# Block order of the first feed-forward layer: token tile 0 in three pieces, and one weight unit converted per block

## The chip, the cores and the metric

The kernel runs on one core of a Trainium2 chip. The metric is the device time of one execution in microseconds. The kernel before takes 804.77 us (median of three runs, 803.89 to 807.13).

## What is computed

Attention in which a query sees only the keys of its own hash bucket, then two feed-forward layers with different activations, on the 1536 tokens that attention puts out:

```python
q_bucket = np.sum((np.einsum('bhsd,dk->bhsk', q, proj) > 0) * 2 ** np.arange(6), axis=-1)   # k_bucket alike
scores = np.where(q_bucket[..., :, None] == k_bucket[..., None, :], scale * q @ k.T, -1e9)
attn_out = softmax(scores) @ v            # batch 2, 8 heads, 768 tokens, head_dim 64
x = attn_out.transpose(0, 2, 1, 3).reshape(1536, 512)
h = x @ w_in;  x = (h * np.cos(h)) @ w_out                 # layer 0: 512 -> 2048 -> 512
h = x @ w_in2; out = (h * np.tanh(log1p(exp(h)))) @ w_out2  # layer 1
```

The weights arrive as 64-bit floats.

## The kernel before, in words

`attention()` runs head by head. `moe()` then runs both layers, feature-major: the tokens are three tiles of 512 (t = 0, 1, 2), d_ff is 16 f-blocks of 128, and each pair of a tile and an f-block is one step of a long list, `uses` (lines 89 to 94), 48 steps for a layer. Tile 0 is finished in the middle of attention; the last pieces of x for tiles 1 and 2 (lines 394 and 397, on GpSimd) come with the last heads.

One pass of the loop at line 681 is called block n here. In it TensorE does h(n), twelve matmuls of w_in by x (line 171), and then o(n-4), twelve matmuls of w_out by the activation of block n-4 (line 667). Every operand is a sum of a high and a low part, so h takes high by high, high by low and low by high. h_mm takes the eight with w_in's high half first and the four with its low half last.

The activation of block n passes ScalarE and VectorE in turn: hs and a from the matmul's result (lines 181 and 183, block n), a on VectorE (193, block n), its absolute value and sine on ScalarE (189 and 190, block n+1), hs times cosine on VectorE (196, block n+1), and the split into gh on ScalarE (204) and gl on VectorE (206), block n+2. o(n) reads gh and gl two blocks later. The four h banks rotate; the four o banks have one buffer each.

A weight unit is w_in or w_out of one f-block: 512 KB of 64-bit floats, loaded by SP into one of five buffers (`load_w`), and converted in three blocks: cg on ScalarE (`conv1`, line 128), three integer operations on VectorE (`conv2`, lines 137, 139 and 142), the high half on ScalarE and the low half on GpSimd (`conv3`, lines 149 and 151). There are four cg buffers; the next unit's cg waits until GpSimd has released one. `due` hands out units in the order of their due times, two per block while n < 12 and one after that, once the slot is free (eight slots for w_in, eight for w_out). Four units, w_in 0 to 3, are converted during attention, and two more at its end. All engines run their queues in the order in which the code emits the instructions: stage_0, ophase, iter1 and split, finish, conv_mid, split_x, conv_next.

A run of steps of one tile adds up in the four o banks. When it ends, `finish` (line 610) empties them: by two copies on VectorE and two on ScalarE into a pa buffer in SBUF (lines 624 and 626), where more f-blocks of the tile are to follow, and by adds on VectorE (632, 641) where the tile is complete. In the kernel before, the runs of a layer are: tile 0, f 0 to 7; tile 1, f 0 to 7; tile 2, all 16; tile 1, f 8 to 15; tile 0, f 8 to 15.

Of the kernel before, what the change touches and what calls it, by code (L numbers as in the profile page):

```python
# [14 lines left out]
ALU = mybir.AluOpType  # L15
# [30 lines left out]
def lsh_moe_kernel(ctx: ExitStack, tc: tile.TileContext, q, k, v, proj, w_in1, w_out1, w_in2, w_out2, cst, out):  # L46
    nc = tc.nc
# [5 lines left out]
    NF = FF // 128  # L53
# [7 lines left out]
    NT3 = B * S // TT  # L61
    GRP = NF // 2

    def f32(ap):
        return ap.bitcast(F32)
# [18 lines left out]
    def slot(pool, part, i):  # L84
        return pool.tile([128, 2, 4, 128], F32R, name=f"w{part}_{i}")

    slots = [[slot(persist, 0, i) for i in range(NEARLY)], []]
    loads = [(wi, wo, f) for wi, wo in ((w_in1, w_out1), (w_in2, w_out2)) for f in range(NF)]
    uses = []
    for m in range(2):  # L90
        ts = list(range(NT3))[:: 1 if m == 0 else -1]
        for g, order in enumerate((ts, ts[::-1])):
            for t in order:
                uses += [(m, t, m * NF + g * GRP + f) for f in range(GRP)]
    NU = len(uses)
    LAG_O = 4
    last_use = {u[2]: n for n, u in enumerate(uses)}
# [26 lines left out]
    def conv1(u, step=None, g=None):  # L124
        if g is None:
            g = cv_p.tile([128, NCT, 128], F32, tag="g", name="cg", bufs=4)
        if step != 1:
            nc.scalar.activation(g, raw_t[u][:, :, :, 1].bitcast(F32), ACTF.Copy, scale=REBIAS)
        return u, g
# [15 lines left out]
    def conv3(st, step=None):  # L145
        (i, part), g = st
        w = slots[part][i % NW]
        if step != 1:
            nc.scalar.activation(w[:, 0], g, ACTF.Copy)  # L149
        if step != 0:  # L150
            nc.gpsimd.tensor_tensor(w[:, 1], g, f32(w[:, 0]), ALU.subtract)  # L151
# [59 lines left out]
    def conv_next(new):  # L211
        for st in pipe[1]:
            conv3(st)
        pipe[1] = pipe[0]
        pipe[0] = [conv1(u) for u in new]

    def conv_mid():
        return itertools.chain(*[conv2(st) for st in pipe[0]])
# [362 lines left out]
    def moe():  # L581
        mctx = ExitStack()
        with mctx:
            w_p = mctx.enter_context(tc.tile_pool(name="wslots", bufs=1))
            pools["g"] = mctx.enter_context(tc.tile_pool(name="g", bufs=4))
            pools["raw"] = mctx.enter_context(tc.tile_pool(name="raw2", bufs=RAWS2))
            ot_p = mctx.enter_context(tc.tile_pool(name="ot", bufs=3))
            pa_p = mctx.enter_context(tc.tile_pool(name="pa", bufs=1))
            ps_h = mctx.enter_context(tc.tile_pool(name="ps_h", bufs=4, space=PSUM))
            ps_o = mctx.enter_context(tc.tile_pool(name="ps_o", bufs=1, space=PSUM))  # L590
            part = [[pa_p.tile([128, TT], F32, name=f"pa{i}_{d}") for d in range(4)] for i in range(2)]
            O = []
            saved = {}
            for x in range(2):
                for i in range(len(slots[x]), NW):
                    slots[x].append(slot(w_p, x, i))
            LAG = LAG_O
            rest = []
            nxt["base"] = nxt["load"]
            for _ in range(RAWS2):  # L600
                load_w()

            def split_x(k):
                for _ in range(k):
                    if rest:
                        xh, xl, y = rest.pop(0)
                        nc.scalar.activation(xh, y, ACTF.Copy)
                        nc.vector.tensor_tensor(xl, y, f32(xh), ALU.subtract)

            def finish(n):  # L610
                m, t, li = uses[n]
                ps = n // GRP % (2 * NT3)
                opens = ps < NT3 - 1
                closes = ps >= NT3
                if not (opens or closes):
                    return
                for d in range(4):
                    s = O[d]
                    if opens:
                        if d == 0:  # L620
                            saved[t] = part[ps]
                        pp = saved[t][d]
                        if d % 2 == 0:
                            nc.vector.tensor_copy(pp, s)
                        else:
                            nc.scalar.activation(pp, s, ACTF.Copy)
                        continue
                    adds = t in saved
                    if m == 0:
                        if adds:  # L630
                            y = saved[t][d]
                            nc.vector.tensor_tensor(y, s, y, ALU.add)
                        else:
                            nc.scalar.activation(XH[t][d], s, ACTF.Copy)
                            nc.vector.tensor_tensor(XL[t][d], s, f32(XH[t][d]), ALU.subtract)
                            continue
                        rest.append((XH[t][d], XL[t][d], y))
                    else:
                        if adds:
                            y = saved[t][d]  # L640
                            nc.vector.tensor_tensor(y, s, y, ALU.add)  # L641
                        else:
                            y = ot_p.tile([128, TT], F32, tag="y", name="y")
                            if d % 2 == 0:
                                nc.vector.tensor_copy(y, s)
                            else:
                                nc.scalar.activation(y, s, ACTF.Copy)
                        b, j = divmod(t * 4 + d, J)
                        dst = out[b * S:b * S + S, :].rearrange("(p j) f -> p j f", j=J)
                        nc.sync.dma_start(out=dst[:, j, :], in_=y)  # L650
                if closes:
                    saved.pop(t, None)

            def ophase(n):
                m, t, li = uses[n]
                ps = n // GRP % (2 * NT3)
                first = n % GRP == 0 and ps != NT3
                last = n % GRP == GRP - 1 and ps != NT3 - 1
                if first:
                    O[:] = [ps_o.tile([128, 512], F32, tag=f"o{d}", name=f"o{d}") for d in range(4)]  # L660
                wo = slots[1][li % NW]
                gh, gl = G.pop(n)
                for d in range(4):
                    ds = slice(d * 128, d * 128 + 128)
                    for x, (wi, g) in enumerate(((0, gh), (1, gh), (0, gl))):
                        lhs, rhs = (wo[:, wi, d, :], g) if m == 0 else (g[:, ds], wo[:, wi].rearrange("p c f -> p (c f)"))
                        nc.tensor.matmul(O[d], lhs, rhs, start=(first and x == 0), stop=(last and x == 2))  # L667

            def due(n, most):
                new = []  # L670
                while nxt["unit"] < len(units):
                    i, part = u = units[nxt["unit"]]
                    ready = i < NW or last_use[i - NW] <= n - LAG * part + 1
                    must = n > 3 and due_at[u] <= n
                    if not ready or (len(new) >= most and not must):
                        break
                    new.append(u)
                    nxt["unit"] += 1
                return new

            for n in range(NU + LAG):
                if n == NU // 2:
                    iter1(n, last=True)
                    nc.scalar.preload_act_table_set("mish")
                if EARLY_H <= n < NU:
                    for _ in h_mm(n, ps_h.tile([128, TT], F32, tag="h", name="h")):
                        pass
                    stage_0(n)
                if n >= LAG:
                    ophase(n - LAG)  # L690
                if EARLY_H <= n < NU // 2:
                    iter1(n)
                elif n >= NU // 2:
                    split(n - 1)
                if n >= LAG and (n - LAG) % GRP == GRP - 1:
                    finish(n - LAG)
                for _ in conv_mid():
                    pass
                split_x(1)
                conv_next(due(n, 2 if n < 12 else 1))  # L700

    with tc.manual_schedule():
        attention()
        moe()
# [28 lines left out]
```

## Time and profile before

| | |
|---|---|
| median of three runs | 804.77 us |
| profiled execution | 804.95 us, of which 803.2 us from the first to the last instruction |
| TensorE busy | 780.2 us (97%) |
| VectorE, ScalarE, GpSimd busy | 538.2, 502.4, 304.3 us |
| attention | to about 262 us |
| the first layer's blocks | from 262.7 us; without a gap from 315 us |
| mean granted clock of TensorE | 0.989 |

A stretch's granted clock is the part of full speed that TensorE was given: 1.00 is 2.4 GHz, 0.50 is 1.2 GHz. Ends of matmuls are modelled, so distances between starts are read. DVE is VectorE, ACT is ScalarE, POOL is GpSimd, PE is TensorE.

### The profile page before, as it was taken

Reading aid. Unit: us, or ns where it says so; the run is one execution under the profiler, and the core shown is the slowest. Engines: PE = TensorE matmul, PEld = TensorE weight load, DVE = VectorE, ACT = ScalarE, POOL = GpSimd, SP = SyncE. Lnnn points to the kernel's source line nnn. Section 1 sums busy time; section 2 is a strip of 40 time slices with the busy share of each in tenths; the row PEclk is TensorE's granted clock in tenths of the full one; section 3 lists DMA queues with packets and bytes.
Section 4 is the critical chain, followed back from the end, with each engine's and each line's share of the span. In section 5 each row is a group of like instructions: output and inputs, shape, how many; then the busy total and the mean of one; then the engine's idle time right before and its main releaser. Section 6 shows DMA issues by size and latency. Waiting matters only on the chain.

```text
span 803.2 us, 11714 instructions
## 1 busy us (share of the span) xinstructions
PE 780.2 (97%) x4020; PEld 666.8 (83%) x4020; DVE 538.2 (67%) x940; ACT 502.4 (63%) x1002; POOL 304.3 (38%) x327
## 2 busy tenths in 40 slices
PE   8999999999999679999999999999999999999998
PEld 5889999999999467888888888888888888888886
DVE  5799899888897698448888546998412666611122
ACT  5899999998987576658777567774322443322120
POOL 4779999999875543002222101232200222200000
PEclk9999999999999889999999999999999999999999
DMA  7454354343320433003233001233200232001011
GB/s 226 102 152 114 104 155 111 104 128 86 84 56 16 162 106 104 1 0 100 84 106 103 29 1 53 79 105 108 76 1 12 94 105 79 0 1 53 0 53 52
DMA packets 38027, 62.36 MB, mean 78 GB/s; under 512 B 3664, under 2 KB 28368, under 8 KB 37968
## 3 DMA queue, kind: packets, MB, share of 16 engines
q1 hardware_dynamic: 37968, 61.63, 26.2%
q8 instruction: 31, 0.51, 0.3%
q14 instruction: 28, 0.23, 0.1%
HBM read 43.13 MB, written 3.15 MB: 58 GB/s over the span
## 4 chain that ended last, share of the span: by engine, by line
PE 60%; DVE 4%; issue 1%; DVEq 0%
PE o L667 31%; PE h L171 29%; DVE cg L142 1%; DVE ct L139 1%; DVE gl L206 1%; DVE ct L137 1%; DVE hs L196 0%; DVE pa L641 0%; DVE a L193 0%; DVEq L142 0%
## 5 line engine op out<-in xcount | busy, mean ns | idle before, releaser
L171 PE MATMUL h<-xh,w 128*128 128x512 f32 x752 | 247.8, 391 | 5.7 <-POOL w L151 5.7
L151 POOL TENSOR_TENSOR w<-cg,w 128x512 fp32r<-128x512 f32 x64 | 88.7, 1388 | 351.1 <-ACT w L149 334.1
L206 DVE TENSOR_TENSOR gl<-hs,gh 128x512 fp32r<-128x512 f32 x96 | 70.8, 737 | 173.8 <-ACT gh L204 173.8
L171 PEld LDWEIGHTS h<-xh,w 128*128 128x128 f32 x752 | 141.9, 189 | 35.9 <-POOL w L151 6.1
L171 PE MATMUL h<-xl,w 128*128 128x512 f32 x376 | 146.3, 389 | 0.0
L178 ACT ACTIVATE hs<-h 128x512 f32<-128x512 f32 x48 | 28.7, 597 | 158.6 <-PE h L171 158.6
L667 PE MATMUL o<-gh,w 128*128 128x512 f32 x384 | 121.4, 398 | 1.5 <-ACT gh L204 1.5
L364 DVE TENSOR_TENSOR pl<-wp,ph 128x384 fp32r<-128x384 f32 x192 | 105.9, 552 | 23.6 <-ACT ph L362 23.0
L667 PE MATMUL o<-w,gh 128*128 128x512 f32 x384 | 118.2, 389 | 0.0
L362 ACT ACTIVATE ph<-wp 128x384 fp32r<-128x384 f32 x192 | 95.8, 500 | 17.6 <-PE wp L358 17.4
L321 PE MATMUL s<-k,q 128*128 128x512 f32 (+1 forms) x384 | 91.7, 361 | 2.2 <-DVE k L475 1.4
L323 DVE TENSOR_REDUCE nm<-s 128x1 f32<-128x768 f32 x96 | 90.1, 939 | 5.4 <-PE s L321 5.4
L667 PEld LDWEIGHTS o<-gh,w 128*128 128x128 f32 x384 | 73.6, 192 | 17.5 <-ACT gh L204 2.2
L667 PEld LDWEIGHTS o<-w,gh 128*128 128x128 f32 x384 | 72.1, 188 | 14.9
L171 PEld LDWEIGHTS h<-xl,w 128*128 128x128 f32 x376 | 70.7, 188 | 14.6
L667 PE MATMUL o<-gl,w 128*128 128x512 f32 x192 | 76.6, 399 | 5.7 <-DVE gl L206 5.7
L667 PE MATMUL o<-w,gl 128*128 128x512 f32 x192 | 74.7, 389 | 0.0
L374 PE MATMUL u<-ph,nv 128*128 128x384 f32 x192 | 72.6, 378 | 0.0
L181 ACT ACTIVATE hs<-h 128x512 f32<-128x512 f32 x46 | 27.5, 597 | 61.9 <-PE h L171 33.1
L374 PE MATMUL u<-pl,nv 128*128 128x384 f32 x192 | 65.0, 338 | 0.3 <-DVE pl L364 0.3
L321 PEld LDWEIGHTS s<-k,q 128*128 128x128 f32 x384 | 58.9, 191 | 7.5 <-DVE k L475 1.5
L204 ACT ACTIVATE gh<-hs 128x512 fp32r<-128x512 f32 x96 | 59.5, 620 | 2.9 <-DVE hs L196 1.4
(101 smaller groups left out, 1427.6 us busy)
## 6 DMA issues: line engine op xcount, KB each, us to landing
wr<-in_moe_w_in_dram SPq DMA_DIRECT2D x32, 512.0 KB, 3.8
wr<-in_moe_w_out_dram SPq DMA_DIRECT2D x32, 512.0 KB, 3.3
rq<-in_q_dram SPq DMA_DIRECT2D x16, 192.0 KB, 2.8
rk<-in_k_dram SPq DMA_DIRECT2D x16, 192.0 KB, 2.6
rv<-in_v_dram SPq DMA_DIRECT2D x16, 192.0 KB, 3.9
q<-q SPq DMA_DIRECT2D x16, 192.0 KB, 2.7
k<-k SPq DMA_DIRECT2D x16, 192.0 KB, 2.7
sh<-us SPq DMA_DIRECT2D x32, 96.0 KB, 2.2
```

Of the source, the lines that this page charges most:

```text
L151: nc.gpsimd.tensor_tensor(w[:, 1], g, f32(w[:, 0]), ALU.subtract)
L171: nc.tensor.matmul(hp, w[:, wi, c, :], X[b][c], start=(i == 0), stop=(i == 3 * NCT - 1))
L178: nc.scalar.activation(hs, hp, ACTF.Mish)
L181: nc.scalar.activation(hs, hp, ACTF.Copy, scale=INV2PI)
L204: nc.scalar.activation(gh, hs, ACTF.Copy)
L206: nc.vector.tensor_tensor(gl, hs, f32(gh), ALU.subtract)
L321: nc.tensor.matmul(s[:, c0:c1], T[a][:, qs], T[c][:, c0:c1], start=(n == 0), stop=(n == 1))
L323: nc.vector.tensor_reduce(nm, s, AX.X, ALU.max, negate=True)
L362: nc.scalar.activation(ph, w, ACTF.Copy)
L364: nc.vector.tensor_tensor(pl, w, f32(ph), ALU.subtract)
L374: nc.tensor.matmul(U[0], lw, x, start=(kt == 0 and n == 0), stop=(kt == J - 1 and n == 1))
L667: nc.tensor.matmul(O[d], lhs, rhs, start=(first and x == 0), stop=(last and x == 2))
```

## The change

The list of steps is written as runs. In layer 0 tile 0's first eight f-blocks are split: tile 0, f 0 to 3; tile 1, f 0 to 7; tile 0, f 4 to 7; tile 2, all; tile 1, f 8 to 15; tile 0, f 8 to 15. Layer 1 keeps its order. `finish` can now add into a pa buffer that already holds a part, and `due` gives one unit per block throughout.

```diff
-    uses = []
-    for m in range(2):
-        ts = list(range(NT3))[:: 1 if m == 0 else -1]
-        for g, order in enumerate((ts, ts[::-1])):
-            for t in order:
-                uses += [(m, t, m * NF + g * GRP + f) for f in range(GRP)]
+    Q = GRP // 2
+    runs = [(0, 0, 0, Q), (0, 1, 0, GRP), (0, 0, Q, GRP), (0, 2, 0, NF), (0, 1, GRP, NF), (0, 0, GRP, NF)]
+    runs += [(1, 2, 0, GRP), (1, 1, 0, GRP), (1, 0, 0, NF), (1, 1, GRP, NF), (1, 2, GRP, NF)]
+    uses, opens_at, closes_at = [], {}, {}
+    for r in runs:
+        m, t, f0, f1 = r
+        opens_at[len(uses)] = r
+        uses += [(m, t, m * NF + f) for f in range(f0, f1)]
+        closes_at[len(uses) - 1] = r
...
             def finish(n):
-                m, t, li = uses[n]
-                ps = n // GRP % (2 * NT3)
-                opens = ps < NT3 - 1
-                closes = ps >= NT3
-                if not (opens or closes):
-                    return
+                m, t, f0, f1 = closes_at[n]
+                adds = t in saved
                 for d in range(4):
                     s = O[d]
-                    if opens:
-                        if d == 0:
-                            saved[t] = part[ps]
+                    if f1 < NF:
+                        if d == 0 and not adds:
+                            saved[t] = part.pop(0)
                         pp = saved[t][d]
-                        if d % 2 == 0:
+                        if adds:
+                            nc.vector.tensor_tensor(pp, s, pp, ALU.add)
+                        elif d % 2 == 0:
                             nc.vector.tensor_copy(pp, s)
                         else:
                             nc.scalar.activation(pp, s, ACTF.Copy)
                         continue
...
-                if closes:
-                    saved.pop(t, None)
+                if f1 == NF and adds:
+                    part.append(saved.pop(t))
...
-                conv_next(due(n, 2 if n < 12 else 1))
+                conv_next(due(n, 1))
```

How this moves the instructions is shown at three places. In the names, xh0 and xl0 are tile 0 of x (high and low part), xh1 and xl1 tile 1; w0_k is the slot of w_in k, w1_k that of w_out k.

TensorE, the end of h(4) and the start of o(0), before:

```order
L171 MATMUL h_5044<-xh0_3_76,w0_4_4906 128x512
L171 MATMUL h_5044<-xl0_3_88,w0_4_4906 128x512
L171 MATMUL h_5044<-xh0_0_73,w0_4_4906 128x512
L171 MATMUL h_5044<-xh0_1_74,w0_4_4906 128x512
L171 MATMUL h_5044<-xh0_2_75,w0_4_4906 128x512
L171 MATMUL h_5044<-xh0_3_76,w0_4_4906 128x512
L667 MATMUL o0_5062<-gh_4973,w1_0_4910 128x512 x2
```

and of the change:

```order
L174 MATMUL h_5014<-xh1_3_80,w0_0_97 128x512
L174 MATMUL h_5014<-xl1_3_92,w0_0_97 128x512
L174 MATMUL h_5014<-xh1_0_77,w0_0_97 128x512
L174 MATMUL h_5014<-xh1_1_78,w0_0_97 128x512
L174 MATMUL h_5014<-xh1_2_79,w0_0_97 128x512
L174 MATMUL h_5014<-xh1_3_80,w0_0_97 128x512
L665 MATMUL o0_5032<-gh_4963,w1_0_4910 128x512 x2
```

h(4) reads tile 1 with w_in 0 in place of tile 0 with w_in 4.

VectorE, from the first conversion after the end of attention (ct and cg are a unit's conversion), before:

```order
L137 TENSOR_SCALAR ct_4934<-cg_4930 128x512
L139 SCALAR_TENSOR_TENSOR ct_4934<-wr_2468,ct_4934 128x512
L142 SCALAR_TENSOR_TENSOR cg_4930<-cg_4930,ct_4934 128x512
L137 TENSOR_SCALAR ct_4940<-cg_4932 128x512
L139 SCALAR_TENSOR_TENSOR ct_4940<-wr_4814,ct_4940 128x512
L142 SCALAR_TENSOR_TENSOR cg_4932<-cg_4932,ct_4940 128x512
L193 SCALAR_TENSOR_TENSOR a_4967<-a_4967,hs_4965 128x512
L206 TENSOR_TENSOR gl_4975<-hs_4759,gh_4973 128x512
L196 SCALAR_TENSOR_TENSOR hs_4844<-hs_4844,b_4848 128x512
```

and of the change:

```order
L140 TENSOR_SCALAR ct_4932<-cg_4930 128x512
L142 SCALAR_TENSOR_TENSOR ct_4932<-wr_2468,ct_4932 128x512
L145 SCALAR_TENSOR_TENSOR cg_4930<-cg_4930,ct_4932 128x512
L196 SCALAR_TENSOR_TENSOR a_4957<-a_4957,hs_4955 128x512
L209 TENSOR_TENSOR gl_4965<-hs_4759,gh_4963 128x512
L199 SCALAR_TENSOR_TENSOR hs_4844<-hs_4844,b_4848 128x512
L140 TENSOR_SCALAR ct_4968<-cg_4940 128x512
L142 SCALAR_TENSOR_TENSOR ct_4968<-wr_4814,ct_4968 128x512
L145 SCALAR_TENSOR_TENSOR cg_4940<-cg_4940,ct_4968 128x512
```

Before, blocks 1 to 5 convert two units each; now blocks 1 to 10 convert one each, so that block 2's a, gl and hs stand one unit further ahead.

VectorE, the first drain of the o banks (block 11 before), before:

```order
L193 SCALAR_TENSOR_TENSOR a_5369<-a_5369,hs_5367 128x512
L206 TENSOR_TENSOR gl_5389<-hs_5291,gh_5387 128x512
L196 SCALAR_TENSOR_TENSOR hs_5329<-hs_5329,b_5333 128x512
L624 COPY pa0_0_4898<-o0_5062 128x512
L624 COPY pa0_2_4900<-o2_5064 128x512
L193 SCALAR_TENSOR_TENSOR a_5411<-a_5411,hs_5409 128x512
```

and of the change (block 7):

```order
L196 SCALAR_TENSOR_TENSOR a_5177<-a_5177,hs_5175 128x512
L209 TENSOR_TENSOR gl_5197<-hs_5079,gh_5195 128x512
L199 SCALAR_TENSOR_TENSOR hs_5127<-hs_5127,b_5131 128x512
L625 COPY pa0_0_4898<-o0_5032 128x512
L625 COPY pa0_2_4900<-o2_5034 128x512
L140 TENSOR_SCALAR ct_5204<-cg_5160 128x512
```

The drain comes four blocks earlier, among the conversions instead of behind them.

## Rows read from the trace of the kernel before

**Rows 1.** The page: busy tenths and granted clock in 40 slices of the span
```profile
PE   8999999999999679999999999999999999999998
...
PEclk9999999999999889999999999999999999999999
```
**Rows 2.** The chain of waits in order of time (start, us, what): its last TensorE piece
```profile
785.74 11.57 PE o L667 x51
```
**Rows 3.** Busy time by stretch: PE, PEld, DVE, ACT, POOL, PEclk, DMA share, GB/s
```profile
280.00:285.00 5.00, 5.00 (x13) 3.80 (x13) 4.79 (x5) 3.14 (x7) 2.96 (x2) 0.50 0.00 0
310.00:315.00 5.00, 3.42 (x16) 2.51 (x15) 4.82 (x5) 2.99 (x6) 2.38 (x2) 1.00 0.54 168
320.00:400.00 80.00, 80.00 (x354) 66.24 (x353) 51.83 (x74) 55.17 (x96) 9.06 (x7) 1.00 0.15 47
```
**Rows 4.** Timeline of TensorE, 276 to 315 us: start, us, what [idle before <-releaser]
```profile
276.08 2.08 PE L171 MATMUL h<-xh,w 128*128 128x512 f32 x4 [5.71 <-POOL w L151]
279.63 1.22 PE L667 MATMUL o<-gh,w 128*128 128x512 f32 x2 [1.48 <-ACT gh L204]
...
289.32 0.50 PE L667 MATMUL o<-gl,w 128*128 128x512 f32 x1 [0.99 <-DVE gl L206]
...
298.21 0.50 PE L667 MATMUL o<-gl,w 128*128 128x512 f32 x1 [3.15 <-DVE gl L206]
...
302.19 0.39 PE L171 MATMUL h<-xh,w 128*128 128x512 f32 x1
...
312.57 0.50 PE L667 MATMUL o<-gl,w 128*128 128x512 f32 x1 [1.58 <-DVE gl L206]
...
314.97 0.39 PE L171 MATMUL h<-xh,w 128*128 128x512 f32 x1
```
**Rows 5.** Timeline of VectorE, a block with two units: its start and the next block's
```profile
303.58 0.68 DVE L193 SCALAR_TENSOR_TENSOR a<-a,hs 128x512 f32<-128x512 f32 x1
...
311.24 0.68 DVE L193 SCALAR_TENSOR_TENSOR a<-a,hs 128x512 f32<-128x512 f32 x1
```
**Rows 6.** Timeline of ScalarE at the end of attention
```profile
274.39 0.67 ACT L128 ACTIVATE cg<-wr 128x512 f32<-128x512 f32 x1 [6.21 <-POOL w L151]
```
**Rows 7.** Timeline of GpSimd at the end of attention
```profile
270.14 2.55 POOL L397 TENSOR_TENSOR xl<-xt,xh 128x512 fp32r<-128x512 f32 x2
272.65 3.37 POOL L151 TENSOR_TENSOR w<-cg,w 128x512 fp32r<-128x512 f32 x2
```
**Rows 8.** Timeline of VectorE there: first and last of six operations in a row
```profile
267.62 1.27 DVE L137 TENSOR_SCALAR ct<-cg 128x512 int32<-128x512 int32 x1
...
273.27 1.63 DVE L142 SCALAR_TENSOR_TENSOR cg<-cg,ct 128x512 int32<-128x512 int32 x1
```
**Rows 9.** Timeline of VectorE, a later block with one unit, and the next one's start
```profile
384.95 0.69 DVE L193 SCALAR_TENSOR_TENSOR a<-a,hs 128x512 f32<-128x512 f32 x1
386.22 0.69 DVE L206 TENSOR_TENSOR gl<-hs,gh 128x512 fp32r<-128x512 f32 x1 [0.58 <-ACT gh L204]
386.83 1.80 DVE L196 SCALAR_TENSOR_TENSOR hs<-hs,b 128x512 f32<-128x512 f32 x1
...
390.40 0.69 DVE L193 SCALAR_TENSOR_TENSOR a<-a,hs 128x512 f32<-128x512 f32 x1
```
**Rows 10.** Timeline of GpSimd in the same block
```profile
386.79 1.29 POOL L151 TENSOR_TENSOR w<-cg,w 128x512 fp32r<-128x512 f32 x1 [4.16 <-ACT w L149]
```
**Rows 11.** Timelines of VectorE and TensorE in block 19 and at the start of o(16)
```profile
375.93 0.69 DVE L196 SCALAR_TENSOR_TENSOR hs<-hs,b 128x512 f32<-128x512 f32 x1
376.53 1.28 DVE L624 COPY pa<-o 128x512 f32<-128x512 f32 x2
...
377.56 0.62 PE L667 MATMUL o<-gh,w 128*128 128x512 f32 x2
```
**Rows 12.** Groups of VectorE's instructions from 345 us on: count, busy us, mean ns
```profile
L632 DVE TENSOR_TENSOR pa<-o,pa 128x512 f32<-128x512 f32 x8 | 5.0, 682 | 0.0
```
**Rows 13.** The page: DMA issues, KB each, median us to landing
```profile
wr<-in_moe_w_in_dram SPq DMA_DIRECT2D x32, 512.0 KB, 3.8
```

More of the change, by code (lines that the diff above doesn't have):

```diff
@@ L627, in finish @@
                         continue
-                    adds = t in saved
                     if m == 0:
@@ L650, in finish @@
                         nc.sync.dma_start(out=dst[:, j, :], in_=y)
-                if closes:
-                    saved.pop(t, None)
+                if f1 == NF and adds:
+                    part.append(saved.pop(t))
             def ophase(n):
                 m, t, li = uses[n]
-                ps = n // GRP % (2 * NT3)
-                first = n % GRP == 0 and ps != NT3
-                last = n % GRP == GRP - 1 and ps != NT3 - 1
+                first, last = n in opens_at, n in closes_at
                 if first:
@@ L694, in moe @@
                     split(n - 1)
-                if n >= LAG and (n - LAG) % GRP == GRP - 1:
+                if n - LAG in closes_at:
                     finish(n - LAG)
```

## The prediction, made before the changed kernel was run

> **What bounds the kernel now.** Start with the page's slices [rows 1]: TensorE is at 9 tenths nearly everywhere; after the first, only the two slices at about 261 to 301 us fall short, where the granted clock also drops. The chain of waits [rows 2] then ends in one unbroken run of TensorE, and the table by stretch [rows 3] shows 80.00 us busy of 80 from 320 to 400. So the change can gain only between the end of attention and 315 us; from there on the program is TensorE's 5.44 us per block: 24 matmuls at 11.57 / 51 = 0.227 us [rows 2], 2.72 for h(n) and 2.72 for o(n-4).
>
> Inside that piece the timeline of TensorE [rows 4] has four stops. h(4) does its eight matmuls with the high half of w_in, then waits 5.71 us for GpSimd's low half of w_in 4. o(0) starts only at 279.63: ScalarE had been held 6.21 us for a free cg buffer [rows 6] and came late to gh(0). Then o(1), o(2) and o(4) wait 0.99, 3.15 and 1.58 us for gl. These are VectorE's: a block with two units takes it 311.24 - 303.58 = 7.66 us [rows 5], more than TensorE's 5.44. The clock adds to it: after the 5.71 us stop it was 0.50 (1.2 GHz) up to 285 [rows 3], and after the 3.15 us stop o(2)'s last ten matmuls took 302.19 - 298.21 = 3.98 us instead of 2.27, a loss of 1.7. The stop of 1.58 us cost no clock: it is 1.00 from 310 to 315 [rows 3]. h(9) starts at 314.97, and everything behind it is fixed to that. I forecast where h(9) starts.
>
> **The change, part by part.**
>
> *Block 4 reads tile 1.* h(4) now needs w_in 0, converted long ago, and tile 1 of x. The last piece of that is the second L397, which ends at 270.14 + 2.55 = 272.69 [rows 7]; it gates the eighth matmul, so five are left: 272.7 + 5 x 0.227 = 273.8. o(0) needs w_out 0's low half, the first of two L151 in 3.37 us from 272.65, thus about 274.3 [rows 7]; o(0) then ends near 276.8. One unit a block takes no cg buffer that is still held, so ScalarE's 6.21 us [rows 6] falls away and gh(0) is ready near 272. The stop here shrinks from 5.71 to about 2.9 us in two pieces. If the clock falls on it, up to some 2 us of TensorE's time go, but they hide under the stop below.
>
> If nothing else waited, h(9) would start eight steps after the end of o(0), at 276.8 + 8 x 2.72 = 298.6: a gain of 16.4 us.
>
> *One unit per block.* VectorE's block is now a, gl, hs and three conversion operations. Later blocks of this kind show the price [rows 9]: 390.40 - 384.95 = 5.45 us, less 0.58 of waiting, 4.87. That is below 5.44, so VectorE gains only 0.57 us a block on TensorE. It holds a collision with GpSimd: hs takes 1.80 us while L151 runs [rows 9, 10], and 0.69 without [rows 11], so 1.11 per unit.
>
> *A drain comes early.* This is the new wait. Tile 0's group now closes after four f-blocks, so at block 7, not 11, VectorE and ScalarE must copy o out before o(4) may start, in the same four PSUM banks. The drain stands on VectorE behind all earlier blocks. Its queue from 270.81 on: one block while GpSimd is busy without a gap, where six operations took 273.27 + 1.63 - 267.62 = 7.3 us [rows 8], to 278.1; four blocks of 4.87 to 297.6; then a, gl, hs and the copy at 0.6 to 0.65 each, 2.5 us, and 1.1 more if a collision falls there: o0 is free between 300.1 and 301.2, say 300.6. TensorE gets there at 276.8 + 7 x 2.72 = 295.8. It waits 4.8 us. ScalarE's two copies come sooner: its seven operations of a block are about 4 us of work (55.17 us for 96 of them [rows 3], 0.57 each), and they stand right behind gh. In the kernel before, the copies at block 19 end about when o(16) starts and cost TensorE nothing [rows 11]; by that row alone the drain would be free and the sum 804.95 - 16.4 + 0.8 = 789.4. The Trainium skill, Perfetto Trace Analysis, "Matmuls" under "Optimizing Tensor Performance", asks that groups rotate through different PSUM banks so that a drain overlaps the next group; the o tiles have one buffer each, and by that rule a drain that is late is paid in full. I side with the queue, because VectorE is behind here and was not there.
>
> A stop of 4.8 us lies between the two that lowered the clock (3.15 and 5.71), so I add the 1.7 of the nearer row. Bounds: 0, and the 3.7 behind the longer stop (the five us from 280 at half speed lose 2.5 [rows 3], h(4)'s last four matmuls 2.08 - 0.91 = 1.2 [rows 4]).
>
> Then h(9) starts at 300.6 + 2.72 + 1.7 = 305.0: 10.0 us sooner than 314.97.
>
> *Four adds more.* Tile 0's second half-group closes at block 15 and is added at block 19: four VectorE adds of 0.68 us [rows 12], 2.7 us of work. In that block before, hs ran without a collision (0.69) because GpSimd came after ScalarE's copies, and the first copy started at 376.53 with o(16) at 377.56 [rows 11]. Now ScalarE has no copies there, so hs meets L151: 1.1 later, the first add ends near 376.53 + 1.1 + 0.68 = 378.3, and o(16) waits about 0.8 us. The rest of the 2.7 us is worked off at 0.57 a block inside the two-block lead that gl has.
>
> *At nothing.* The copies of tile 1 at block 15: no units are left to convert then, so VectorE is up to date. The order of loads changes (w_out before w_in 4 to 7), but each lands in about 3.8 us [rows 13] and is issued at least four conversions, over 19 us, before it is needed; without that cover one late load would cost up to those 3.8. Block 16 and on, and all of layer 2, keep their order; the two pa buffers only swap owners.
>
> **Sum.** 804.95 - 10.0 + 0.8 = 795.8 us against the profiled execution, which lies 0.18 above the median shown (804.77).
>
> **Rivals.**
>
> 1. *The drain is nearly free.* If collisions are rarer than one a block, as for operations that do not meet L151, VectorE's block is 4.87 - 1.1 = 3.8 and four of them gain 4.4 us: the stop shrinks to under 1 us and the clock stays up. h(9) at about 299; 788.6 to 791.5. For it: GpSimd's 1.29 us must fall on the right operation. Against: the ordinary block of [rows 9] has the collision.
> 2. *VectorE is slower still.* A second block beside a busy GpSimd (its two L151 run into it) costs 7.3 instead of 4.87, 2.4 more; or a collision costs all of L151, 1.29 [rows 10] instead of 1.11, 0.9 more over five blocks. With up to 2 us more of lost clock: 797.5 to 800.7. For it: the six operations of [rows 8]. Against: the single collision in [rows 9]. The Trainium skill, SBUF — State Buffer, "Who interferes with whom", says that the loser of the port pair that VectorE and GpSimd share blocks for the whole other instruction; by that rule the 1.29 would hold and the sum be 796.7. The rows come to 1.11, a little less.
> 3. *No change that can be seen*: the wait at h(4) goes but block 4 to 8 stay as slow as before, because a chain from ScalarE to VectorE and back, not VectorE's amount of work, sets them. Gain only of the first stop, 2.9 us, to 802. Against: ScalarE's 4 us of a block [rows 3] are less than VectorE's 4.87.
> 4. *Slower: the clock does not come back.* If the stop at h(4) drops TensorE to 1.2 GHz and short waits in every block keep it there, each step takes 5.44 us: h(9) at 273.8 + 9 x 5.44 = 322.8, 7.8 after 314.97, and with the 0.8 it is 813.4. It decides once half speed lasts over 2 x 16.4 = 33 us. Against: before, after a longer stop, full speed was back by 285, under 10 us later.
>
> **How the numbers follow.** A measurement of this kernel can tell about 0.5%, 4.0 us, from no change. My forecast (793 to 797.5): 0.50. Rival 1: 0.22. Rival 2: 0.19. Rival 3: 0.06. Rival 4: 0.03. Faster than 800.75 are the first three: 0.91; within 0.5%: 0.06; slower: 0.03. The range 789 to 800 leaves out the far ends of rivals 1 and 2 and all of 3 and 4.
>
> **What would show it.** In the profile after: h's longest wait for GpSimd near 3 us, with xl ahead of it, not L151; no wait of ScalarE for a cg buffer beyond 2 us before gh(0); VectorE without idle time from 268 to 300; at block 7 one stop of TensorE of 3 to 6 us that ends with VectorE's copy of o0; a dip of the granted clock right behind it; h(9) near 305; a wait of under 1 us at o(16). I am wrong if TensorE also waits for gl in blocks 5 to 7 by over 1 us each, if the stop at block 7 is under 1 us, or if anything behind block 20 moves.

## The result, and the profile after

The changed kernel takes 796.99 us (median of four runs, 796.35 to 798.01); the kernel before, run beside it, 804.46 us (median of four). The ratio is 0.9902, 95% interval 0.9877 to 0.9926. The profiled execution takes 796.35 us, its span is 794.6 us, and TensorE's mean granted clock is 0.994.

On the page, TensorE's busy tenths in 40 slices. After the first, and but for the last, two slices are left at 8 tenths, at about 258 to 278 and 298 to 318 us; [rows 1] had 6 and 7 at 261 to 301 us:

```profile
PE   7999999999999898999999999999999999999998
```

The timeline of TensorE from 268 to 308 us (start, us, what, [idle before <-releaser]):

```profile
269.52 0.49 PE L174 MATMUL h<-xh,w 128*128 128x512 f32 x1 [0.55 <-POOL xh L397]
272.32 0.50 PE L174 MATMUL h<-xl,w 128*128 128x512 f32 x1 [2.30 <-POOL xl L400]
272.65 1.17 PE L174 MATMUL h<-xh,w 128*128 128x512 f32 x4
273.62 1.18 PE L665 MATMUL o<-gh,w 128*128 128x512 f32 x2
...
277.98 0.39 PE L174 MATMUL h<-xh,w 128*128 128x512 f32 x1
...
301.10 1.19 PE L665 MATMUL o<-gh,w 128*128 128x512 f32 x2 [3.89 <-DVE pa L625]
...
305.39 0.39 PE L174 MATMUL h<-xh,w 128*128 128x512 f32 x1
```

Compare [rows 4]. At h(4) GpSimd is waited for twice, 0.55 and 2.30 us, and the name is xl, tile 1 of x, where it was w, the low half of w_in 4, for 5.71 us. The waits for gl at o(1), o(2) and o(4) are gone: between 277.98 and 301.10 - 3.89 = 297.21 us TensorE waits for nothing. One stop is new, 3.89 us at o(4), ended by VectorE's copy of o0. h(9) starts at 305.39; before, at 314.97.

TensorE's clock in two stretches (columns as in [rows 3]):

```profile
273.00:277.00 4.00, 4.00 (x12) 2.86 (x11) 3.96 (x3) 2.98 (x6) 4.00 (x3) 0.57 0.02 6
...
301.00:305.00 4.00, 3.90 (x11) 3.12 (x12) 3.86 (x7) 2.07 (x4) 0.86 (x1) 0.60 0.20 55
```

Behind each stop it falls to 0.57 and 0.60 of full speed over four us, and that lasts about one group of twelve matmuls: o(0) takes 277.98 - 273.62 = 4.36 us and o(4) 305.39 - 301.10 = 4.29 us, in place of 2.72.

VectorE from 266.89 us on; it has no idle time up to the copies of o:

```profile
266.89 1.29 DVE L140 TENSOR_SCALAR ct<-cg 128x512 int32<-128x512 int32 x1
...
269.93 1.76 DVE L196 SCALAR_TENSOR_TENSOR a<-a,hs 128x512 f32<-128x512 f32 x1
...
278.28 0.68 DVE L196 SCALAR_TENSOR_TENSOR a<-a,hs 128x512 f32<-128x512 f32 x1
...
279.49 1.78 DVE L199 SCALAR_TENSOR_TENSOR hs<-hs,b 128x512 f32<-128x512 f32 x1
...
297.38 0.68 DVE L196 SCALAR_TENSOR_TENSOR a<-a,hs 128x512 f32<-128x512 f32 x1
...
298.58 1.77 DVE L199 SCALAR_TENSOR_TENSOR hs<-hs,b 128x512 f32<-128x512 f32 x1
300.27 1.27 DVE L625 COPY pa<-o 128x512 f32<-128x512 f32 x2
```

A row of a begins each block: the first block runs from 269.93 to 278.28 (8.35 us), the next four to 297.38 (4.78 each). In each of them hs takes 1.78 us, beside GpSimd's subtraction (e4 below takes that away). GpSimd's own timeline shows what runs beside the first block: the low part of x and then three subtractions in a row, to 277.09:

```profile
269.44 2.83 POOL L400 TENSOR_TENSOR xl<-xt,xh 128x512 fp32r<-128x512 f32 x2
272.23 4.86 POOL L154 TENSOR_TENSOR w<-cg,w 128x512 fp32r<-128x512 f32 x3
279.11 1.62 POOL L154 TENSOR_TENSOR w<-cg,w 128x512 fp32r<-128x512 f32 x1 [2.02 <-ACT w L152]
```

ScalarE has gh(0) at 270.24, before its one wait for a cg buffer, which is 2.61 us in place of the first 6.21 [rows 6]; its two copies at block 7 are done at 297.94, VectorE's at 301.54:

```profile
270.24 0.61 ACT L207 ACTIVATE gh<-hs 128x512 fp32r<-128x512 f32 x1
...
273.99 0.69 ACT L131 ACTIVATE cg<-wr 128x512 f32<-128x512 f32 x1 [2.61 <-POOL w L154]
...
296.88 1.06 ACT L627 ACTIVATE pa<-o 128x512 f32<-128x512 f32 x2
```

At o(16), TensorE's timeline shows the second new wait:

```profile
368.89 0.70 PE L665 MATMUL o<-gh,w 128*128 128x512 f32 x2 [0.76 <-DVE pa L623]
```

VectorE's shows the four adds, behind an hs that is stretched to 1.80:

```profile
366.35 1.80 DVE L199 SCALAR_TENSOR_TENSOR hs<-hs,b 128x512 f32<-128x512 f32 x1
368.07 2.47 DVE L623 TENSOR_TENSOR pa<-o,pa 128x512 f32<-128x512 f32 x4
```

The counterpart of [rows 2], in the chain of waits:

```profile
777.14 11.57 PE o L665 x51
```

It starts 785.74 - 777.14 = 8.60 us sooner, as much as the span is shorter. The account: 9.58 us at h(9) less 0.76 at o(16) is 8.82; the last 0.2 us are in no single row. 0.73 of the 9.58 isn't the change's: attention ended that much sooner in this execution (VectorE's first row 266.89, against 267.62 in [rows 8]). That end moves from execution to execution: over the eleven profiled ones of this document TensorE's last wait in attention ends between 261.25 us (this one, the earliest) and 262.32, in both orders.

### The profile page after: what moved, and what is told of

Read it like the earlier page. It is cut to its first block, busy times and chain, and to the rows that moved or that the text cites. A ratio compares the mean times of both kernels' runs of the same rounds, so it can differ in the third digit from the quotient of the medians.

```text
span 794.6 us, 11720 instructions
## 1 busy us (share of the span) xinstructions
PE 777.2 (98%) x4020; PEld 665.5 (84%) x4020; DVE 541.8 (68%) x944; ACT 502.1 (63%) x1002; POOL 305.3 (38%) x327
## 3 DMA queue, kind: packets, MB, share of 16 engines
HBM read 43.13 MB, written 3.15 MB: 58 GB/s over the span
## 4 chain that ended last, share of the span: by engine, by line
PE 59%; DVE 3%; ACT 1%; issue 1%; DVEq 0%; ACTq 0%
PE o L665 30%; PE h L174 29%; DVE hs L199 2%; DVE pa L641 0%; ACT gh L207 0%; ACT hs L184 0%; ACT a L186 0%; DVE gl L209 0%; ACT a L192 0%; DVE ct L142 0%; DVE cg L145 0%; DVE ct L140 0%; ACT pa L627 0%; ACT cg L131 0%; DVE pa L623 0%
## 5 line engine op out<-in xcount | busy, mean ns | idle before, releaser
L209 DVE TENSOR_TENSOR gl<-hs,gh 128x512 fp32r<-128x512 f32 x96 | 69.0, 719 | 168.6 <-ACT gh L207 168.6
L199 DVE SCALAR_TENSOR_TENSOR hs<-hs,b 128x512 f32<-128x512 f32 x48 | 64.9, 1352 | 1.8 <-ACT b L193 1.8
```

The lines of the kernel that those rows point to most:

```text
L199: nc.vector.scalar_tensor_tensor(hs1, hs1, TWO_PI, b1, ALU.mult, ALU.mult)
L209: nc.vector.tensor_tensor(gl, hs, f32(gh), ALU.subtract)
```

## The experiments

Nine more kernels, and three questions: are both parts of the change needed; is the stop at o(4) VectorE's queue; and what makes that queue long.

| kernel | order | units per block | low half on | other | median us | ratio to before, 95% |
|---|---|---|---|---|---|---|
| before | old | two | GpSimd | | 804.46 to 805.25 | 1 |
| changed | new | one | GpSimd | | 796.99 | 0.9877 to 0.9926 |
| e1_rate_alone | old | one | GpSimd | | 800.63 | 0.9909 to 0.9954 |
| e2_order_alone | new | two | GpSimd | | 813.54 | 1.0075 to 1.0112 |
| e3_drain_on_act | new | one | GpSimd | drain on ScalarE | 792.02 | 0.9813 to 0.9843 |
| e4_low_on_dve | new | one | VectorE | | 790.31 | 0.9794 to 0.9832 |
| e5_rate_low_on_dve | old | one | VectorE | | 803.43 | 0.9961 to 0.9985 |
| e6_x_first | new | one | GpSimd | tile 1 of x first | 796.83 | 0.9876 to 0.9914 |
| e7_low_on_dve_x_first | new | one | VectorE | tile 1 of x first | 789.60 | 0.9789 to 0.9836 |
| e8_all_three | new | one | VectorE | both | 788.50 | 0.9774 to 0.9822 |
| e9_before_low_on_dve | old | two | VectorE | | 807.69 | 1.0015 to 1.0038 |

The changed kernel's 796.99 was timed apart from e1 to e9. The median of the kernel before moved by 0.8 us from one occasion to another (804.46 to 805.25), so a difference to 796.99 is good to about that.

### The two parts apart: e1 and e2

e1, on the kernel before:

```diff
-                conv_next(due(n, 2 if n < 12 else 1))
+                conv_next(due(n, 1))
```

> The order of the kernel before, with one weight unit per block. Theory (VectorE's two units per block were the cost, the new order only shortens the first stop and pays for it with an early drain): the 5.7 us stop at h(4) and the half clock behind it stay, o(0) follows h(4) near 278 and no matmul waits for gl after that; no drain at block 7, no wait at o(16); h(9) near 306 and about 796 us, the same as the changed kernel within 2 us. Rival A (the order is what gains, because h(4) no longer waits for w_in 4): 801 us or more, since that stop stays. Rival B (units now come too late for the order of before, which needs two a block): TensorE waits for L151 or L149 in blocks 5 to 8, 803 us or more.

Measured 800.63 us, 4.6 above the theory and just below rival A. TensorE's stops in the profiled execution (798.26 us, the fastest of the four), from 262 to 330 us:

```profile
276.06 2.08 PE L171 MATMUL h<-xh,w 128*128 128x512 f32 x4 [6.00 <-POOL w L151]
...
289.00 0.50 PE L171 MATMUL h<-xh,w 128*128 128x512 f32 x1 [1.02 <-ACT w L149]
...
296.11 0.50 PE L171 MATMUL h<-xh,w 128*128 128x512 f32 x1 [1.38 <-ACT w L149]
...
299.11 1.20 PE L171 MATMUL h<-xh,w 128*128 128x512 f32 x4 [0.89 <-POOL w L151]
```

The waits for gl are gone, so the rate does what the prediction gave it. The stop at h(4) stays whole, so that part belongs to the order. And three waits for units are new, as rival B has it: the old order wants w_in 4 to 7 and w_out 0 to 3 in blocks 4 to 7, and one unit per block is too few for it. (`due` hands out a unit beyond its limit when the unit's due time has come. In e1 and e5 this gives two units in block 4; in the changed kernel it never happens.)

e2, on the changed kernel, is the same line the other way round:

```diff
-                conv_next(due(n, 1))
+                conv_next(due(n, 2 if n < 12 else 1))
```

> The new order with two units per block while n < 12. Theory: four units more stand on VectorE ahead of the copy at block 7, 4 x 2.95 us, so o(4) starts near 313 and h(9) near 317; about 808 us, slower than before. Rival A (the order gains): 797 us or less. Rival B (the drain is set by something other than VectorE's queue): the stop at o(4) stays near 4 us, about 797 us.

Measured 813.54 us, slower than before and 5.5 above what was expected. Its stops at h(4), at o(0) and behind:

```profile
272.95 0.50 PE L174 MATMUL h<-xl,w 128*128 128x512 f32 x1 [2.02 <-POOL xl L400]
...
279.86 1.22 PE L665 MATMUL o<-gh,w 128*128 128x512 f32 x2 [5.48 <-ACT gh L207]
...
289.57 0.50 PE L665 MATMUL o<-gl,w 128*128 128x512 f32 x1 [0.88 <-DVE gl L209]
...
298.46 0.50 PE L665 MATMUL o<-gl,w 128*128 128x512 f32 x1 [3.15 <-DVE gl L209]
...
317.89 1.19 PE L665 MATMUL o<-gh,w 128*128 128x512 f32 x2 [7.08 <-ACT a L186]
```

h(4) is served early, as forecast, but the time is lost again one step later: with two units in block 1 ScalarE is held for a cg buffer as in [rows 6] (here 6.26 us), and o(0) waits 5.48 us for gh(0). The first two waits for gl of [rows 4] are there too (0.88 and 3.15 us), and at o(4) the early drain, behind two units a block, costs 7.08 us. The row names ScalarE's a, which no matmul of o reads; I read VectorE's first copy of o as what o(4) waits for. Rows of VectorE:

```profile
278.05 0.69 DVE L196 SCALAR_TENSOR_TENSOR a<-a,hs 128x512 f32<-128x512 f32 x1 [2.91 <-ACT a L186]
...
317.06 1.28 DVE L625 COPY pa<-o 128x512 f32<-128x512 f32 x2
```

The forecast missed two things. VectorE waits for ScalarE too, 2.91 us for a and then 1.10 for gh, and its copies come that much later; and behind the stop o(4) runs at half speed to its end (5.23 us in place of 2.72, a loss of 2.5, where the forecast had 1.7).

So the parts don't add. The rate alone is worth 4.6 us, the order alone costs 8.3, both together gain 7.5 (each against the kernel before that was timed beside it).

### The stop at o(4): e3

The four copies of block 7 all on ScalarE, which in the changed kernel was done with its two at 297.94:

```diff
-                        elif d % 2 == 0:
+                        elif d % 2 == 0 and f1 != Q:
                             nc.vector.tensor_copy(pp, s)
```

> The changed kernel with all four copies of the drain at block 7 on ScalarE. Theory (VectorE's queue holds that drain, and the stop lowers the clock): ScalarE reaches the copies near 297, the stop at o(4) shrinks from 3.9 to under 1 us, no half clock behind it; about 5.5 us less than the changed kernel, 791.5. Rival (ScalarE's four copies make it late, or VectorE's lag shows at the next gl instead): the stop moves to o(4) to o(6) and the time stays within 2 us of 797.

Measured 792.02 us. ScalarE's copies:

```profile
296.87 2.04 ACT L627 ACTIVATE pa<-o 128x512 f32<-128x512 f32 x4
```

TensorE at o(4):

```profile
297.70 0.63 PE L665 MATMUL o<-gh,w 128*128 128x512 f32 x2
...
298.39 0.62 PE L665 MATMUL o<-gh,w 128*128 128x512 f32 x2
```

o(4) follows h(8) without a stop and at full speed (the two rows are 0.69 us apart, three matmuls). The wait of 0.76 us at o(16) stays. The four banks are the same; only the queue in front of the copies is another. This shows that the late drain, with its half clock, cost about 5 us, and that it was late for VectorE's queue.

### What makes VectorE's queue long: e4

The low half of a unit is subtracted on VectorE, except for the units converted during attention (step 1). VectorE gets one operation more per unit, and GpSimd has nothing left to do from 272.86 us on, behind the last of x:

```diff
-            nc.gpsimd.tensor_tensor(w[:, 1], g, f32(w[:, 0]), ALU.subtract)
+            eng = nc.gpsimd if step == 1 else nc.vector
+            eng.tensor_tensor(w[:, 1], g, f32(w[:, 0]), ALU.subtract)
```

> The changed kernel with the low half of the units of the feed-forward part subtracted on VectorE (0.7 us) and not on GpSimd. Theory (each L151 on GpSimd costs VectorE a collision of 1.1 us): hs takes 0.69 in every block, VectorE's block falls from 4.78 to about 4.4 us though it does one operation more, the copy at block 7 comes about 5 us sooner and the stop at o(4) is under 1 us; about 790.5. Rival (the long hs is not GpSimd's doing): VectorE's block is 4.8 + 0.6 = 5.4 us, the drain comes 3 us later or more, 800 us.

Measured 790.31 us. Three rows of a block of VectorE, and the start of the next:

```profile
281.14 0.68 DVE L197 SCALAR_TENSOR_TENSOR a<-a,hs 128x512 f32<-128x512 f32 x1
...
282.34 0.69 DVE L200 SCALAR_TENSOR_TENSOR hs<-hs,b 128x512 f32<-128x512 f32 x1
...
284.73 0.69 DVE L155 TENSOR_TENSOR w<-cg,w 128x512 fp32r<-128x512 f32 x1
285.33 0.68 DVE L197 SCALAR_TENSOR_TENSOR a<-a,hs 128x512 f32<-128x512 f32 x1
```

Seven operations take 4.19 us where six took 4.78: hs is back at 0.69, and the added operation (L155) takes 285.33 - 284.73 = 0.60. So GpSimd's subtraction did cost VectorE 1.78 - 0.69 = 1.09 us a block, more than doing the work itself. The first block, 8.35 us in the changed kernel, takes 4.72 (272.21 to 276.93). The copies of o begin at 296.55, 3.7 us sooner and not 5, since VectorE waits 0.92 us for gh in front of them; that is soon enough. There is no stop at o(4) or o(16) any more. The half clock behind h(4)'s stop is still there (0.57 of full speed from 273 to 277 us), and here no later stop covers it.

### Is the order needed then: e5 and e9

e5 is the kernel before with e1's and e4's edits; e9 with e4's alone.

> The order of before (tile 0 with eight f-blocks in a row), one unit per block, and the low half of a unit (from block 0 on) subtracted on VectorE in place of GpSimd. It asks whether the new order is needed at all once GpSimd is out of the conversion. If order matters only through GpSimd's queue at the end of attention (theory A): w_in 4's low half is ready near 272.3, the stop at h(4) falls from 5.7 to about 2 us, nothing else waits, the drain stays at block 11, 789 to 791 us. If the order matters through the number of units that it wants (theory B: tile 0's f-blocks 4 to 7 need a new w_in and a new w_out in each of blocks 4 to 7 while one unit per block is converted): waits of TensorE for ScalarE's high half or VectorE's low half at h(5) to h(7), about 1 us each and with a loss of clock, 793 to 799 us. I lean to B, because the order with one unit per block and the subtraction on GpSimd had three such waits (1.02, 1.38 and 0.89 us).

Measured 803.43 us: theory B, and worse than its range. Nine waits for units lie between 273 and 322 us, 13 us in sum, among them

```profile
278.48 0.50 PE L172 MATMUL h<-xh,w 128*128 128x512 f32 x1 [1.01 <-ACT w L149]
...
292.41 1.79 PE L172 MATMUL h<-xh,w 128*128 128x512 f32 x4 [3.12 <-DVE w L152]
```

The stop at h(4) is short (2.48 us), so w_in 4 itself comes soon; the old order asks too early for the units behind it. Six of the nine waits are for VectorE's low half, 10.5 us of the 13. Against e1 (old order, one unit per block, low half on GpSimd) e4's edit makes the kernel 2.8 us slower (800.63 to 803.43). Why these waits are longer than e1's, no run takes apart.

> The kernel before with one thing changed: the low half of a unit (from block 0 on) subtracted on VectorE in place of GpSimd; order and two units per block stay. It asks how much of the gain of the two edits together (790.3 us) comes without the new order. VectorE's block with two units would be a, gl, hs at 0.6 and twice 2.4 of conversion, 6.6 us instead of 7.66, still over TensorE's 5.44. Theory (VectorE's queue): the stop at h(4) falls from 5.7 to 2 to 2.5 us, ScalarE has no wait of 6 us for a cg buffer, gl still waits in blocks 5 to 7, 3 to 4 us in sum instead of 5.7; 797 to 801 us, so that the order is worth 7 us or more beyond it. Rival (the collision with GpSimd was the whole of VectorE's lateness): no wait for gl of 1 us, 789 to 794 us.

Measured 807.69 us, slower than before, and outside both forecasts. The stop at h(4) is 4.66 us, not 2 to 2.5, and TensorE waits not for gl but for gh, 1.49 to 2.36 us at each of o(0) to o(3), 8.4 in sum:

```profile
297.72 0.73 PE L668 MATMUL o<-gh,w 128*128 128x512 f32 x2 [2.36 <-ACT gh L205]
```

Its ScalarE in one block:

```profile
287.80 1.14 ACT L149 ACTIVATE w<-cg 128x512 fp32r<-128x512 f32 x2
293.55 1.26 ACT L128 ACTIVATE cg<-wr 128x512 f32<-128x512 f32 x2 [4.61 <-DVE w L152]
```

Its VectorE, from one row of a to the next block's:

```profile
286.14 0.69 DVE L194 SCALAR_TENSOR_TENSOR a<-a,hs 128x512 f32<-128x512 f32 x1 [1.79 <-ACT a L184]
...
295.91 0.69 DVE L194 SCALAR_TENSOR_TENSOR a<-a,hs 128x512 f32<-128x512 f32 x1 [1.79 <-ACT a L184]
```

VectorE's block is 295.91 - 286.14 = 9.77 us, not 6.6, and hardly for work: 1.79 us are a wait for a and 1.10 one for gh, both ScalarE's. ScalarE's cg of the next two units waits until VectorE has done the low halves of the last two, and VectorE's a then waits for ScalarE. This is the chain from ScalarE to VectorE and back of the prediction's rival 3: it exists, with two units per block and the last reader of a cg buffer on VectorE; with one unit it doesn't close (ScalarE's cg waits for no buffer in e4 or e5). So e4's edit, worth 6.7 us in the changed kernel (796.99 to 790.31), costs 2.6 in the kernel before. But the chain alone doesn't decide between gain and loss: the same edit costs 2.8 in the old order with one unit too (e1 to e5), where ScalarE waits for no cg buffer. The new order with two units and the low half on VectorE was not run.

### The stop at h(4): e6, e7, e8

e6 is the changed kernel with the last pieces of x on GpSimd in the other order:

```diff
-big, rest = ((0, 0, TT), (1, 0, S - TT)) if b == 0 else ((2, 0, TT), (1, S - TT, TT))
+big, rest = ((0, 0, TT), (1, 0, S - TT)) if b == 0 else ((1, S - TT, TT), (2, 0, TT))
```

> The changed kernel, with GpSimd's last pieces of x in the other order: tile 1's quarter (256 columns) ahead of tile 2's (512 columns). It takes the wait for xl at h(4) down alone. Theory (VectorE's queue up to the copy of o0 at block 7 sets where o(4) starts, so the stop at h(4) is covered): the stop at h(4) falls from 2.9 to about 1 us, TensorE comes to o(4) up to 2 us sooner and waits that much longer there (3.9 becomes 4 to 6 us), copy of o0 near 300.3 as before, time 796 to 798 us, no change to the changed kernel. Rival (the stop at h(4) and its half clock are paid in full): 793 to 795 us.

Measured 796.83 us: no difference to the changed kernel. TensorE's stops:

```profile
271.11 0.50 PE L174 MATMUL h<-xl,w 128*128 128x512 f32 x1 [1.43 <-POOL xl L400]
...
274.48 0.50 PE L665 MATMUL o<-gh,w 128*128 128x512 f32 x1 [1.72 <-POOL w L154]
...
301.59 1.19 PE L665 MATMUL o<-gh,w 128*128 128x512 f32 x2 [5.26 <-DVE pa L625]
```

The waits of 0.55 and 2.30 us have become 1.43 and 1.72. The second, for w_out 0's low half at o(0), wasn't in the forecast of about 1 us. o(0) runs at full speed, and TensorE comes to o(4) at 296.33, 0.88 sooner; there it waits 5.26 in place of 3.89 (attention ended 0.47 later here, and VectorE's copies start 0.49 later). So the half clock behind h(4) was covered, as the prediction had it.

e7 has e4's edit and e6's; e8 these two and e3's.

> Low half on VectorE and tile 1's pieces of x first, together. With the low half on VectorE TensorE no longer waits at o(4), so here the stop at h(4) should count: it falls from 3.2 to about 1 us and its half clock (1.7 us) goes. VectorE's queue then becomes the next limit: copies of o near 296 while TensorE comes near 295, a wait of up to 1 us. Theory: 788 to 789.5 us, 1 to 2 us below the 790.3 of the low half on VectorE alone. Rival (gl of block 0 or the drain takes it all back): 790 us or more.

> Low half on VectorE, tile 1's pieces of x first, and the four copies at block 7 all on ScalarE. If in the kernel with the first two VectorE's copy holds o(4), this one is up to 1 us faster: 787 to 788.5 us, without a stop at o(4). If no wait is left there, ScalarE's two copies more change nothing, or delay gh by 1 us: 788 to 790 us.

Measured 789.60 and 788.50 us, e7 0.1 above the theory's range and e8 at its upper end. In e7 the copy of o0 is late by 0.69 us, as expected; in e8 that is gone, and two waits are left between 270 us and the end:

```profile
271.49 0.50 PE L175 MATMUL h<-xl,w 128*128 128x512 f32 x1 [1.63 <-POOL xl L401]
...
274.34 0.50 PE L666 MATMUL o<-gl,w 128*128 128x512 f32 x1 [0.97 <-DVE gl L210]
```

The intervals of e4, e7 and e8 overlap; that e8 is the fastest of them rests on the spans of the profiled executions (788.5, 787.5, 786.7 us) and on the waits that each lacks. All three beat the changed kernel by 6.7 us or more.

## Why the prediction was right, point by point

Forecast 795.8, profiled execution 796.35, median 796.99.

- *Block 4 reads tile 1.* Right: the wait is for xl, and gh(0) isn't held. That the sum agrees (2.85 us in two pieces, forecast 2.9) is in part luck: the second piece was to be w_out 0's low half at o(0), about 0.5 us, and was xh, 0.55. That low half shows as a wait at o(0) in e6 (1.72 us). Nor is every cg buffer free: one wait of 2.61 us is left, but it stands behind gh(0). e1 and e2 share the credit out: without the order the stop stays (6.00), without the rate gh(0) is held (5.48).
- *End of o(0).* Forecast 276.8; measured 277.98, though attention ended 0.73 sooner. The clock fell behind this stop, 1.6 us in o(0). The prediction allowed up to 2 us for it and said that it would hide under the later stop; e6 shows that it did.
- *VectorE's first block.* The worst-sized term: forecast 7.3, measured 8.35. The 7.3 was six operations beside a busy GpSimd in the trace of before; here GpSimd had a third subtraction in the same run, and ran on to 277.09 (in e4, with GpSimd free from 272.86 on, the block takes 4.72). The sooner end of attention (0.73) and shorter blocks behind it (0.36) took that back. The 0.73 is luck: without it the profiled execution would have taken about 797.1 us, near the median of 796.99.
- *One unit per block.* Forecast 4.87 with a collision of 1.11; measured 4.78 and 1.09. The Trainium skill, SBUF — State Buffer, "Who interferes with whom", was weighed at 1.29, the whole other instruction; the trace shows 1.09, and GpSimd's own operation takes 1.62 where it starts during VectorE's gl (1.29 in [rows 10]).
- *The drain.* Forecast: o0 free at 300.6, TensorE there at 295.8, a wait of 4.8. Measured: the copies start at 300.27, o(4) at 301.10, TensorE there at 297.21, 3.89. o0 came free near the late end of the bounds because a collision did fall on the last hs (1.77). The wait is shorter because TensorE came later. e3 shows the mechanism by itself. The rule that the prediction named (Perfetto Trace Analysis, "Matmuls" under "Optimizing Tensor Performance", in the Trainium skill) holds here: with one buffer for each o bank, TensorE paid the whole lateness, 3.89 us.
- *The clock behind it.* Forecast 1.7; measured 4.29 - 2.72 = 1.57.
- *h(9).* Forecast 305.0, measured 305.39.
- *Adds at block 19.* Forecast 0.8, measured 0.76, with hs at 1.80 ahead of them.
- *At nothing.* No wait for a load, none at block 15 or behind block 20.
- *Rivals.* Rival 1 (collisions rarer) and rival 2 (a second long block) didn't come; one us of rival 2's kind did, in the first block. Rival 4 didn't: full speed was back within one group of matmuls each time. Rival 3 didn't, since VectorE had no idle time here; its chain shows in e9.

The prediction has two slips that bear on nothing in the result: it counts four stops before 315 us and names five waits, and rival 4's 813.4 counts from the median (804.77), where the other sums count from the profiled execution (it would be 813.6).

What the prediction didn't see: that either part alone brings a wait of its own, and that the collision that it counted as a price can be taken away. It put the gain without any other wait at 16.4 us; e8, in which o(4) and o(16) no longer wait, gains 804.80 - 788.50 = 16.3. That they agree to 0.1 us is chance: e8's waits at h(4) and o(0) are 1.63 and 0.97 us, the sum's 2.9 in all.

## What to carry to other kernels

Before a change that has two parts, ask of each what the other part needs: here an order that wants fewer units early and a rate that gives fewer belong together, and either alone left or made a wait (800.63 and 813.54 against 796.99). When a drain moves to an earlier place, look at what stands in front of it on its engine; the engine with the shorter queue was the better place here. Where an operation on one engine lengthens those of another, compare that with the cost of doing it there, but look first at who releases its buffer and who waits for its result: the same move gained 6.7 us in the new order, and in the old one it lost 2.8 with one unit per block and 2.6 with two.

## What was not expected of the hardware

- VectorE does seven operations in less time than six with GpSimd's subtraction beside them (4.19 against 4.78 us).
- The clock fell behind a stop of 2.30 us with one of 0.55 shortly ahead of it (0.57 from 273 to 277 us), as it did behind 3.89 (0.60). Behind e6's stops of 1.43 and 1.72 us it did not (1.00 from 272 to 277 us): o(0)'s steps of three matmuls start at 275.05, 275.74 and 276.43 us there, 0.69 apart, as at full speed (three times 0.227 is 0.68).
